# A decode attention kernel: K of each block in one transfer through three slots, the middle slot transposed first

## The chip, the cores and the metric

The kernel runs on one core of a Trainium2 chip. The core has a matrix engine (PE, with its weight loads listed as PEld), a vector engine (DVE), a scalar engine (ACT), a general engine (POOL, hardly used here) and a sync engine (SP) that issues the transfers from HBM; 16 DMA engines carry them. Each engine works through its own instructions in order and waits on semaphores for the others. The metric is the device time of one execution in microseconds; before the change it is 1268.74 us, the median of three runs (1267.89 to 1269.64).

## What is computed

One query token goes through a gated sum of two branches. Branch A is attention with 16 query heads over 8 K/V heads, 65,536 cached positions each, head size 256, and a product with `wo`. Branch B is a small mixer (layer norm, gelu, two vectors `w1`, `w2`). Cut to what matters:

```python
g = sigmoid((x * gate_w).sum(-1, keepdims=True))
q = (x @ wq).reshape(1, 1, 16, 256).transpose(0, 2, 1, 3)
k = repeat(k_cache, 2, axis=1); v = repeat(v_cache, 2, axis=1)
scores = einsum("bhqd,bhkd->bhqk", q, k) * 256 ** -0.5
o = einsum("bhqk,bhkd->bhqd", softmax(scores), v)
a = o.transpose(0, 2, 1, 3).reshape(1, 1, 4096) @ wo
u = gelu(einsum("bsd,sf->bdf", layernorm(x), w1) + b1)
b = (einsum("bdf,fs->bds", u, w2) + b2).transpose(0, 2, 1)
return g * a + (1 - g) * b
```

All arrays are bfloat16. K and V together are 537 MB, and each of their bytes is used by the two query heads of one K/V head only.

## The kernel before

The caches are cut into 32 blocks of 16,384 positions (8 MB of K and 8 MB of V each), four blocks to a K/V head. A position's row lies on one of 128 partitions; each partition holds 128 positions of a block, 64 KB of K and 64 KB of V, contiguous in HBM.

Per block: K lies in two tiles of 32 KB per partition, `kn0` and `kn1` (`k_tiles`), V in one tile `vt` of 64 KB. DVE transposes K in eight steps of 16 positions (`transposes`, line 384) into one of two tiles `kT`; after each step PE makes eight matmuls with the query placed in `qz` (`scores`, line 392) and gathers the scores of the block in one PSUM tile. After the eighth, `softmax` (line 444) follows on DVE, PE and ACT: the block's maximum, the running maximum, the exponentials `p_sb`, their transposition `pT`, the running sum `lsum` (line 488). Then 64 matmuls of `products` (line 412) multiply `pT` with V, and `accumulate` (line 493) adds them to `acc`.

The blocks 0 to 29 run in a loop of 15 passes of two blocks each, `e` = 0 and 1 (line 560). Every pass also loads one row set of `wo` (224 KB, `load_wo`) into `wo_sb[:, 1]`. At the end of the odd block, `denominators` and `head_end` turn `acc` into a head's output, multiply it with `wo_sb`, and ACT copies `wo_sb[:, 1]` to `wo_sb[:, 0]`; `turn` switches constants. `place_q` puts the next pair's query in place in the odd block's softmax. The blocks 30 and 31 are written out after the loop (line 581): their transfers are cut into pieces, and the last block's V goes into the K tiles in eight pieces (`load_v_last`), the last of which are small; its products are split between PE matmuls of two forms (`pv` into `pv_last`, and `columns`, line 437), and the result is multiplied with `wo_sb` (line 639).

The function `seq` fixes the order of each engine's instructions as written. All large transfers are issued by SP in program order into one queue, which the DMA engines serve in order. The order in a pass is V of the even block, K halves of the odd block, `wo`, V of the odd block, K halves of the next even block. An issue of K waits until the transposes have read the tile half that it overwrites; an issue of V waits until the products of the block before have read `vt`.

The loop uses staggered semaphores: its body has four stages, parted by `tc.stage_boundary()`, and an engine may enter a stage only when every engine has signalled that it is done with the stage two before. An engine signals this at the start of the following stage, unless the program names an earlier place with `tc.previous_stage_wait(engine)`; the kernel before names none. Stage 0 holds the even block's transposes, scores and V load, stage 1 its softmax and products and the next K loads; stages 2 and 3 hold the same for the odd block. SP passes through these stages like the others, so its K loads of stage 1 wait for all engines' signals about stage 3, and so on.

Before the loop, the query is made from `wq` (which lies in `vt` for that time), and the mixer's 14 gelu rows `gel` lie in the two `kT` tiles.

Of the kernel before, what the change touches and what calls it, by code (L numbers as in the profile page):

```python
# [8 lines left out]
FP32 = mybir.dt.float32  # L9
# [22 lines left out]
def kernel(  # L32
# [28 lines left out]
    def seq(ins):  # L61
        e = ins.ins.engine
        if e in last:
            tc.add_manual_dep(
                ins.ins,
                last[e],
                mybir.DependencyInfo(
                    mybir.DependencyClass.NoSync, mybir.DependencyReason.DATA
                ),
                reason="program order",  # L70
            )
        last[e] = ins.ins.name
        return ins
# [4 lines left out]
    psum = ctx.enter_context(tc.tile_pool(name="psum", bufs=1, space=bass.MemoryType.PSUM))  # L78


    kvpool.tile([128, 4096 - 128], mybir.dt.uint8, name="fill")
    k_tiles = [kvpool.tile([128, KP, DH], BF16, name=f"kn{i}") for i in range(2)]
    vt = kvpool.tile([128, VP, DH], BF16, name="vt")
    kT_tiles = [kvpool.tile([128, NJ, NW, 32, 2], BF16, name=f"kT{i}") for i in range(2)]
    p_sb = work.tile([128, 512], BF16)
    pT_tiles = [work.tile([128, 512], BF16, name=f"pT{i}") for i in range(2)]
    wo_sb = const.tile([128, REP, 2, D], BF16)
# [21 lines left out]
    gel = [  # L109
        kT_tiles[b % 2][:].rearrange("p j w k c -> p (j w k c)")[:, b // 2 * D:(b // 2 + 1) * D]  # L110
        for b in range(NF)
    ]

    flat = {}
    for name, cache in (("k", A_k_cache), ("v", A_v_cache)):
# [2 lines left out]
    def rows(name, n):  # L118
        return flat[name][bass.ds(n, 1)].rearrange("o p j d -> (o p) j d")

    def load_k(n, h, pieces=((0, KP),)):
        for j0, j1 in pieces:
            seq(nc.sync.dma_start(
                out=k_tiles[h][:, j0:j1, :],
                in_=rows("k", n)[:, h * KP + j0:h * KP + j1, :],
            ))

    def load_v(n, j0=0, j1=VP):
        seq(nc.sync.dma_start(out=vt[:, j0:j1, :], in_=rows("v", n)[:, j0:j1, :]))  # L129

    def pairs(ap):
        return ap.rearrange("p (i j) d -> p i j d", i=2)

    LAST = ((0, 32), (32, 64), (64, 80), (80, 96), (96, 112), (112, 120), (120, 124), (124, 128))

    def load_wo(h, r):
        seq(nc.sync.dma_start(
            out=wo_sb[:, r],
            in_=A_wo.rearrange("(h p c) n -> h p c n", p=128, c=2)[bass.ds(h, 1)].rearrange(
                "o p c n -> (o p) c n"  # L140
            ),
        ))

    def load_v_last(n):
        for j0, j1 in LAST:
            seq(nc.sync.dma_start(  # L146
                out=k_tiles[j0 // KP][:, j0 % KP:(j1 - 1) % KP + 1, :],
                in_=rows("v", n)[:, j0:j1, :],
            ))

# [5 lines left out]
    with nc.allow_non_contiguous_dma(reason="short rows"):  # L156
# [78 lines left out]
    sdev = work.tile([128, 1], FP32)  # L235
    rstd = work.tile([128, 1], FP32)
    ntmp = work.tile([128, 1], FP32)
    xf = work.tile([128, D], FP32)
    h_bc = work.tile([128, D], FP32)
    w1f = const.tile([128, NF], FP32)  # L240
    b1f = const.tile([128, NF], FP32)
    seq(nc.vector.tensor_copy(out=xf[:], in_=sm_ps[:, 0:D]))
    seq(nc.vector.bn_stats(out=stats[:], in_=xf[:]))
# [8 lines left out]
    for _ in range(2):  # L252
# [4 lines left out]
        ))  # L257
        seq(nc.vector.tensor_tensor(out=rstd[:], in0=rstd[:], in1=ntmp[:], op=ALU.mult))
    seq(nc.vector.tensor_scalar(
        out=h_bc[:], in0=xf[:], scalar1=mv[:, 0:1], scalar2=rstd[:, 0:1],  # L260
        op0=ALU.subtract, op1=ALU.mult,
    ))
    for b in range(NF):
        seq(nc.scalar.activation(
            out=gel[b], in_=h_bc[:], func=ACT.Gelu_apprx_tanh,
            scale=w1f[:, b:b + 1], bias=b1f[:, b:b + 1],
        ))

# [42 lines left out]
            ))  # L311

    place_q(0)
    zt = work.tile([1, D], FP32)
    z = const.tile([1, 1], FP32)
    ez = const.tile([1, 1], FP32)
    gate = const.tile([1, 1], FP32)
# [2 lines left out]
    rest = const.tile([1, D], FP32)  # L320

    def gate_sum():
        seq(nc.vector.tensor_tensor(out=zt[:], in0=xf[0:1, :], in1=gw[:], op=ALU.mult))
        seq(nc.vector.tensor_reduce(out=z[:], in_=zt[:], op=ALU.add, axis=AXIS.X))
        seq(nc.scalar.activation(out=ez[:], in_=z[:], func=ACT.Exp, scale=-1.0))

    def mixer_sum():
# [52 lines left out]
            out=ends[:], in0=ends[:], scalar1=-1.0, scalar2=1.0, op0=ALU.mult, op1=ALU.add  # L380
        ))

    def transposes(i):
        seq(nc.vector.transpose(  # L384
            out=kT_tiles[i % 2][:].rearrange("p j w k c -> p (j w k c)").bitcast(FP32),
            in_=k_tiles[i // 4][:, i % 4 * NJ:(i % 4 + 1) * NJ, :].rearrange("p j d -> p (j d)").bitcast(FP32),
        ))

    def scores(e, i):
        for w in range(NW):  # L390
            for c in range(2):
                seq(nc.tensor.matmul(  # L392
                    sc_tiles[e][:, :],
                    lhsT=qz[:, 2 * w + c, 2 * (NI - i):2 * (NI - i) + 128],
                    rhs=kT_tiles[i % 2][:, :, w, :, c],
                    start=(i == 0 and w == 0 and c == 0),
                    stop=(i == NI - 1 and w == NW - 1 and c == 1),
                ))
# [34 lines left out]
    def columns(j0, j1):  # L433
        for j in range(j0, j1):
            i, jj = divmod(j, NJ)
            for c in range(2):
                seq(nc.tensor.matmul(
                    o_last[:, c, :],
                    lhsT=k_tiles[j // KP][:, j % KP, :].rearrange("p (d c) -> p c d", c=2)[:, c, :],
                    rhs=pT_tiles[L % 2][:, 32 * jj + REP * i:32 * jj + REP * (i + 1)],  # L440
                    start=(j == KP and c == 0), stop=(j == VP - 1), skip_group_check=True,
                ))
# [176 lines left out]

    for ip in range(2):  # L620
        pv(L, ip, tile=k_tiles[0][:, 32 * ip:32 * (ip + 1), :], dst=pv_last, last_ip=1)
    accumulate(L % 2, pv_last)
    columns(64, 80)
    for c in range(2):
# [53 lines left out]
```

## Time and profile before

| what | value |
|---|---|
| median of three runs | 1268.74 us |
| the profiled execution's own time | 1268.93 us |
| its span (first to last instruction) | 1267.1 us |
| bytes read from HBM, rate over the span | 544.45 MB, 430 GB/s |
| PE busy | 806.4 us (64%) |
| DVE busy | 707.7 us (56%) |
| ACT busy | 58.6 us (5%) |
| mean granted PE clock | 0.807 |
| score matmuls, line 392 | 2048, 419 ns each |
| K transposes, line 384 | 256, 2283 ns each |
| product matmuls, line 412 | 1968, 526 ns each |
| K loads in halves (4 MB) | 63, median 27.3 us from issue to landing |
| V loads (8 MB) | 30, median 31.1 us from issue to landing |
| `wo` loads (224 KB) | 17, median 27.3 us from issue to landing |

The span lies inside the time of the execution; some 1.8 us lie around it. Matmuls overlap in the array, so the mean of one is longer than the distance between two. A landing time counts from the issue, so it holds the wait for the transfers ahead in the queue. In a row of the timeline the columns are start, duration, engine, line, operation, output and inputs, count, and in brackets the idle time before it with what ended it.

### The profile page before, as it was taken

How to read it: one execution, taken by the hardware profiler on the slowest of the kernel's cores; microseconds unless marked ns; L12 is line 12 of the kernel's file. 1: busy time of each engine (PE TensorE's matmuls, PEld its weight loads, DVE VectorE, ACT ScalarE, POOL GpSimd, SP SyncE). 2: the span in 40 equal slices, each digit the busy share in tenths (PEclk: the TensorE clock that was granted, in tenths of full speed). 3: DMA queues.
4: the chain of work that ended last, by engine and by line, in shares of the span. 5: the costliest groups of instructions: out<-in, count | busy, mean ns of one | idle time of the engine just before them, and what ended most of it. 6: DMA issues, size and time to landing. Idle time of an engine off the chain costs nothing.

```text
span 1267.1 us, 12204 instructions
## 1 busy us (share of the span) xinstructions
PE 806.4 (64%) x4689; PEld 321.2 (25%) x4689; DVE 707.7 (56%) x754; ACT 58.6 (5%) x131; POOL 1.7 (0%) x7
## 2 busy tenths in 40 slices
PE   3767665766656566566675675755657665676676
PEld 1222222222222222222222222222222222222223
DVE  4566545565445665456654556644566544665483
ACT  4000000000000000000000000000000000000000
POOL 0000000000000000000000000000000000000000
PEclk9888778788778787787877788777888778787687
DMA  9999999999999999999999999999999999999998
GB/s 413 414 437 444 429 439 418 435 432 446 434 418 437 431 450 432 432 420 432 449 432 435 418 433 434 445 435 418 438 430 447 435 430 424 430 446 435 418 419 343
DMA packets 18306, 544.59 MB, mean 430 GB/s; under 512 B 2421, under 2 KB 4600, under 8 KB 5112
## 3 DMA queue, kind: packets, MB, share of 16 engines
q1 hardware_dynamic: 17858, 544.45, 99.6%
q8 instruction: 6, 0.10, 0.0%
q10 hardware_dynamic: 438, 0.01, 0.0%
q14 instruction: 4, 0.03, 0.0%
HBM read 544.45 MB, written 0.00 MB: 430 GB/s over the span
## 4 chain that ended last, share of the span: by engine, by line
DMA 75%; issue 18%; PE 2%; DVE 2%; SPq 1%; ACT 0%; DVEq 0%
DMA vt<-in_A_v_cache_dram 73%; DMA kn<-in_A_v_cache_dram 2%; DVE kT L384 1%; PE sc L392 1%; PE pv_ps L412 1%; SPq L560 0%; SPq L129 0%; PE hd_ps L528 0%; PE f L639 0%; ACT p_sb L480 0%; DVE acc L493 0%; SPq L146 0%; DVE rmax L449 0%; DVE y_sb L339 0%; PE hd_ps L514 0%
## 5 line engine op out<-in xcount | busy, mean ns | idle before, releaser
L392 PE MATMUL sc<-kT,qz 128*128 128x512 bf16 x2048 | 550.9, 419 | 217.3 <-DVE kT L384 217.1
L384 DVE STREAM_TRANSPOSE kT<-kn 128x2048 f32<-128x2048 f32 x256 | 571.2, 2283 | 109.4 <-DMA kn<-in_A_k_cache_dram 52.6
L392 PEld LDWEIGHTS <-qz 128*128 128x128 bf16 x2048 | 212.7, 104 | 556.1 <-issue 379.4
L412 PE MATMUL pv_ps<-vt,pT 128*4 128x512 bf16 x1968 | 172.5, 526 | 129.0 <-DMA vt<-in_A_v_cache_dram 127.2
L493 DVE SCALAR_TENSOR_TENSOR acc<-acc,al,pv_ps 128x512 f32<-128x512 f32 x31 | 23.2, 748 | 266.5 <-PE pv_ps L412 266.5
L412 PEld LDWEIGHTS <-pT 128*4 128x4 bf16 x2000 | 58.7, 108 | 235.1 <-issue 190.0
L480 ACT ACTIVATE p_sb<-sc,nb 128x512 bf16<-128x512 f32 x32 | 22.0, 687 | 975.6 <-DVE nb L476 975.6
L449 DVE TENSOR_REDUCE rmax<-sc 128x1 f32<-128x512 f32 x32 | 22.1, 692 | 63.6 <-PE sc L392 63.6
L487 DVE STREAM_TRANSPOSE pT<-p_sb 128x512 bf16<-128x512 bf16 x32 | 22.8, 711 | 27.1 <-ACT p_sb L480 27.1
L499 PE MATMUL hd_ps<-lsum,same 128*128 128x1 f32 x30 | 7.4, 315 | 28.8 <-DVE lsum L488 28.8
L467 PE MATMUL sm_ps<-mrun,ones_f 1*128 1x2 f32 x64 | 12.1, 256 | 21.2 <-DVE mrun L466 12.9
L453 PE MATMUL sm_ps<-ident_f,rmax 128*1 128x128 f32 x32 | 8.6, 270 | 24.5 <-DVE rmax L449 24.5
L533 ACT COPY wo_sb<-wo_sb 128x896 bf16<-128x896 bf16 x15 | 14.1, 937 | 199.1 <-PE hd_ps L528 199.1
L514 PE MATMUL hd_ps<-esc,acc 128*128 128x2 f32 x60 | 9.5, 263 | 14.1 <-DVE acc L493 14.1
L528 PE MATMUL hd_ps<-wo_sb,oT 128*1 128x448 bf16 x60 | 17.9, 393 | 0.0
L532 DVE TENSOR_TENSOR a_acc<-a_acc,hd_ps 1x448 f32<-1x448 f32 x15 | 9.1, 608 | 14.5 <-PE hd_ps L528 14.5
L467 PEld LDWEIGHTS sm_ps<-mrun,ones_f 1*128 1x128 f32 x64 | 9.4, 182 | 27.4 <-DVE mrun L466 16.3
L499 PEld LDWEIGHTS hd_ps<-lsum,same 128*128 128x128 f32 x30 | 6.1, 253 | 30.1 <-DVE lsum L488 30.1
L514 PEld LDWEIGHTS hd_ps<-esc,acc 128*128 128x128 f32 x60 | 8.2, 196 | 21.6 <-DVE acc L493 21.6
L476 DVE CUSTOM_DVE_ANT_0 junk<-sm_ps,nval 128x2 f32<-128x2 f32 x32 | 5.1, 160 | 14.0 <-PE sm_ps L467 14.0
L453 PEld LDWEIGHTS sm_ps<-ident_f,rmax 128*1 128x1 f32 x32 | 2.5, 79 | 40.2 <-DVE rmax L449 40.2
L308 DVE COPY qz<-qq 32x16 bf16 (+1 forms) x64 | 10.5, 164 | 1.4
(114 smaller groups left out, 149.5 us busy)
## 6 DMA issues: line engine op xcount, KB each, us to landing
kn<-in_A_k_cache_dram SPq DMA_DIRECT2D x63, 4096.0 KB, 27.3
vt<-in_A_v_cache_dram SPq DMA_DIRECT2D x1, 5120.0 KB
kn<-in_A_k_cache_dram SPq DMA_DIRECT2D x2, 2048.0 KB, 11.9
kn<-in_A_v_cache_dram SPq DMA_DIRECT2D x2, 2048.0 KB, 20.9
wo_sb<-in_A_wo_dram SPq DMA_DIRECT2D x17, 224.0 KB, 27.3
vt<-in_A_wq_dram SPq DMA_DIRECT2D x1, 3072.0 KB, 10.3
vt<-in_A_v_cache_dram SPq DMA_DIRECT2D x1, 3072.0 KB
kn<-in_A_v_cache_dram SPq DMA_DIRECT2D x3, 1024.0 KB, 20.4
```

The source lines that it names most:

```text
L384: seq(nc.vector.transpose(out=kT_tiles[i % 2][:].rearrange("p j w k c -> p (j w k c)").bitcast(FP32), in_=k_tiles[i // 4][:, i % 4 * NJ:(i ...
L392: seq(nc.tensor.matmul(sc_tiles[e][:, :], lhsT=qz[:, 2 * w + c, 2 * (NI - i):2 * (NI - i) + 128], rhs=kT_tiles[i % 2][:, :, w, :, c], star ...
L412: seq(nc.tensor.matmul(dst[32 * grp:32 * grp + 2 * REP, :, :], lhsT=pT[:, 32 * jj + 2 * REP * ip:32 * jj + 2 * REP * (ip + 1)], rhs=pairs( ...
L449: seq(nc.vector.tensor_reduce(out=rmax[:], in_=sc_ps[:, :], op=ALU.max, axis=AXIS.X))
L467: seq(nc.tensor.matmul(sm_ps[:, 128:128 + REP], lhsT=ones_f[0:1, :], rhs=mrun[0:1, :], start=True, stop=True))
L480: seq(nc.scalar.activation(out=p_sb[:, :], in_=sc_ps[:, :], func=ACT.Exp, scale=scale, bias=nb[:, 0:1], accum_out=den[:, 0:1],))
L487: seq(nc.vector.transpose(out=pT[:, :], in_=p_sb[:, :]))
L493: seq(nc.vector.scalar_tensor_tensor(out=acc[:], in0=acc[:], scalar=al_tiles[e][:, 0:1], in1=src[:, :, :], op0=ALU.mult, op1=ALU.add,))
L499: seq(nc.tensor.matmul(hd_ps[:, 460:461], lhsT=same[:].rearrange("p a r -> p (a r)"), rhs=lsum[:, 0:1], start=True, stop=True,))
L514: seq(nc.tensor.matmul(o_ps[c], lhsT=acc[:, e, :].rearrange("p (d c) -> p c d", c=2)[:, c, :], rhs=weights[:, e, :], start=(start and e == ...
L528: seq(nc.tensor.matmul(a_ps, lhsT=oT[:, c, r:r + 1], rhs=wo_sb[:, r, c, :], start=(r == 0 and c == 0), stop=(r == REP - 1 and c == 1),))
L533: seq(nc.scalar.copy(out=wo_sb[:, 0], in_=wo_sb[:, 1]))
```

## The change

K now has 96 KB per partition: one tile `k_all` with three slots of 32 KB. An even block lies in slots 0 and 1, an odd block in slots 1 and 2. Each block in the loop is loaded by one transfer of 8 MB (`load_k_whole`) in place of two. An even block transposes slot 1 first and then slot 0 (`UPPER_FIRST`), an odd block slot 1 and then slot 2, so that slot 1, the middle one, is free after four transposes in both. The start and stop flags of the score matmuls follow that order.

The signals between the stages are placed by name: in stages 0 and 2, ACT's before the block and PE's and DVE's after the first step of transposes and scores; in stages 1 and 3, DVE's and ACT's after the softmax and PE's after the first quarter of the products.

Room for the third slot is made by laying the early values (`gel`, `xf`, `h_bc`, `zt`) into slot 2, and `wo_sb` into the padding in front of the K tile. Before the loop, block 0 is loaded with slot 1 first (in two pieces) and slot 0 second.

After the loop, block 30 lies in slots 0 and 1 and is transposed slot 1 first; block 31's first half goes to slot 2 and its second half to slot 1; block 31's V pieces go to slots 0 and 2. The mixer's tail and the gate's column come after block 30's softmax in place of between its transposes. Only head 15's rows of `wo` are loaded at the end; head 14's stay from the loop's last copy.

```diff
-    k_tiles = [kvpool.tile([128, KP, DH], BF16, name=f"kn{i}") for i in range(2)]
+    k_all = kvpool.tile([128, 3 * KP, DH], BF16, name="k_all")
+    slots = [k_all[:, i * KP:(i + 1) * KP, :] for i in range(3)]
...
+    early = slots[2].rearrange("p j d -> p (j d)")
+    gel = [early[:, b * D:(b + 1) * D] for b in range(NF)]
...
+    def load_k_whole(n, slot):
+        seq(nc.sync.dma_start(out=k_all[:, slot * KP:(slot + 2) * KP, :], in_=rows("k", n)))
...
+    v_half = [slots[0], slots[2]]
...
-    load_k(0, 0, ((0, 32), (32, KP)))
-    load_k(0, 1)
+    load_k(0, 1, 1, ((0, 32), (32, KP)))
+    load_k(0, 0, 0)
...
+    FORWARD = tuple(range(NI))
+    UPPER_FIRST = FORWARD[NI // 2:] + FORWARD[:NI // 2]
...
-    def score_block(e, hooks={}):
-        for i in range(NI):
-            transposes(i)
-            scores(e, i)
-            if i in hooks:
-                hooks[i]()
+    def score_block(e, pair, hooks={}, order=FORWARD):
+        for k, i in enumerate(order):
+            transposes(pair, i)
+            scores(e, i, k == 0, k == NI - 1)
+            if k in hooks:
+                hooks[k]()
...
     def products(e):
         for ip in range(NI // 2):
             pv(e, ip)
+            if ip == 0:
+                tc.previous_stage_wait(mybir.EngineType.PE)
         accumulate(e)
...
+    def early_signals(i):
+        def both():
+            tc.previous_stage_wait(mybir.EngineType.PE)
+            tc.previous_stage_wait(mybir.EngineType.DVE)
+        return {i: both}
+
     with tc.For_i(0, HQ - 1, 1, iteration_sync="staggered") as t:
         for e in range(2):
             if e:
                 tc.stage_boundary()
-            score_block(e)
+            tc.previous_stage_wait(mybir.EngineType.Activation)
+            score_block(
+                e, (e, e + 1), early_signals(0), FORWARD if e else UPPER_FIRST
+            )
             load_v(2 * t + e)
             tc.stage_boundary()
-            load_k(2 * t + e + 1, 0)
-            load_k(2 * t + e + 1, 1)
             if e == 0:
+                load_k_whole(2 * t + 1, 1)
                 load_wo(t, 1)
                 softmax(e, may_begin=True)
+                tc.previous_stage_wait(mybir.EngineType.DVE)
+                tc.previous_stage_wait(mybir.EngineType.Activation)
                 products(e)
             else:
+                load_k_whole(2 * t + 2, 0)
                 softmax(e, pair=t + 1)
+                tc.previous_stage_wait(mybir.EngineType.DVE)
+                tc.previous_stage_wait(mybir.EngineType.Activation)
                 denominators()
                 products(e)
                 head_end()
...
         if n < L:
-            score_block(n % 2, {1: mixer_tail, 2: gate_column})
+            score_block(0, (0, 1), order=UPPER_FIRST)
         else:
-            score_block(n % 2, {1: result_base, 2: lambda: pv(L - 1, 0), 3: lambda: pv_one(L - 1, 2)})
+            score_block(1, (2, 1), {1: result_base, 2: lambda: pv(L - 1, 0), 3: lambda: pv_one(L - 1, 2)})
         if n == L - 1:
             load_v(n, 0, 48)
-            load_k(L, 0)
-            load_k(L, 1)
+            load_k(L, 0, 2)
+            load_k(L, 1, 1)
             load_v(n, 48, VP)
         else:
             load_v_last(L)
-            for h in range(HQ - REP, HQ):
-                load_wo(h, h - (HQ - REP))
+            load_wo(HQ - 1, 1)
         if n < L:
             softmax(n % 2)
+            mixer_tail()
+            gate_column()
```

More of the change, by code (lines that the diff above doesn't have):

```diff
@@ L78 @@
     psum = ctx.enter_context(tc.tile_pool(name="psum", bufs=1, space=bass.MemoryType.PSUM))
-    kvpool.tile([128, 4096 - 128], mybir.dt.uint8, name="fill")
-    k_tiles = [kvpool.tile([128, KP, DH], BF16, name=f"kn{i}") for i in range(2)]
+    wo_sb = kvpool.tile([128, REP, 2, D], BF16, name="wo_sb")
+    kvpool.tile([128, 4096 - 128 - REP * 2 * D * 2], mybir.dt.uint8, name="fill")
+    k_all = kvpool.tile([128, 3 * KP, DH], BF16, name="k_all")
+    slots = [k_all[:, i * KP:(i + 1) * KP, :] for i in range(3)]
     vt = kvpool.tile([128, VP, DH], BF16, name="vt")
@@ L108 @@
     wq_t = vt[:, 48:56, :].rearrange("p a b -> p (a b)")
[L109 to L112, printed above, removed]
+    early = slots[2].rearrange("p j d -> p (j d)")
+    gel = [early[:, b * D:(b + 1) * D] for b in range(NF)]
+    early_f = early[:, NF * D:].bitcast(FP32)
+    xf, h_bc, zt = [early_f[:, i * D:(i + 1) * D] for i in range(3)]
+    zt = zt[0:1, :]
     flat = {}
@@ L146, in load_v_last @@
             seq(nc.sync.dma_start(
-                out=k_tiles[j0 // KP][:, j0 % KP:(j1 - 1) % KP + 1, :],
+                out=v_half[j0 // KP][:, j0 % KP:(j1 - 1) % KP + 1, :],
                 in_=rows("v", n)[:, j0:j1, :],
@@ L237 @@
     ntmp = work.tile([128, 1], FP32)
-    xf = work.tile([128, D], FP32)
-    h_bc = work.tile([128, D], FP32)
     w1f = const.tile([128, NF], FP32)
     b1f = const.tile([128, NF], FP32)
-    seq(nc.vector.tensor_copy(out=xf[:], in_=sm_ps[:, 0:D]))
-    seq(nc.vector.bn_stats(out=stats[:], in_=xf[:]))
+    seq(nc.vector.tensor_copy(out=xf, in_=sm_ps[:, 0:D]))
+    seq(nc.vector.bn_stats(out=stats[:], in_=xf))
     seq(nc.vector.bn_aggr(out=mv[:], in_=stats[:]))
@@ L259 @@
     seq(nc.vector.tensor_scalar(
-        out=h_bc[:], in0=xf[:], scalar1=mv[:, 0:1], scalar2=rstd[:, 0:1],
+        out=h_bc, in0=xf, scalar1=mv[:, 0:1], scalar2=rstd[:, 0:1],
         op0=ALU.subtract, op1=ALU.mult,
@@ L264 @@
         seq(nc.scalar.activation(
-            out=gel[b], in_=h_bc[:], func=ACT.Gelu_apprx_tanh,
+            out=gel[b], in_=h_bc, func=ACT.Gelu_apprx_tanh,
             scale=w1f[:, b:b + 1], bias=b1f[:, b:b + 1],
@@ L313 @@
     place_q(0)
-    zt = work.tile([1, D], FP32)
     z = const.tile([1, 1], FP32)
@@ L322, in gate_sum @@
     def gate_sum():
-        seq(nc.vector.tensor_tensor(out=zt[:], in0=xf[0:1, :], in1=gw[:], op=ALU.mult))
-        seq(nc.vector.tensor_reduce(out=z[:], in_=zt[:], op=ALU.add, axis=AXIS.X))
+        seq(nc.vector.tensor_tensor(out=zt, in0=xf[0:1, :], in1=gw[:], op=ALU.mult))
+        seq(nc.vector.tensor_reduce(out=z[:], in_=zt, op=ALU.add, axis=AXIS.X))
         seq(nc.scalar.activation(out=ez[:], in_=z[:], func=ACT.Exp, scale=-1.0))
@@ L381, in turn, with transposes, scores @@
         ))
-    def transposes(i):
+    FORWARD = tuple(range(NI))
+    UPPER_FIRST = FORWARD[NI // 2:] + FORWARD[:NI // 2]
+    def transposes(pair, i):
         seq(nc.vector.transpose(
             out=kT_tiles[i % 2][:].rearrange("p j w k c -> p (j w k c)").bitcast(FP32),
-            in_=k_tiles[i // 4][:, i % 4 * NJ:(i % 4 + 1) * NJ, :].rearrange("p j d -> p (j d)").bitcast(FP32),
+            in_=slots[pair[i // 4]][:, i % 4 * NJ:(i % 4 + 1) * NJ, :].rearrange("p j d -> p (j d)").bitcast(FP32),
         ))
-    def scores(e, i):
+    def scores(e, i, begin, end):
         for w in range(NW):
@@ L395, in scores @@
                     rhs=kT_tiles[i % 2][:, :, w, :, c],
-                    start=(i == 0 and w == 0 and c == 0),
-                    stop=(i == NI - 1 and w == NW - 1 and c == 1),
-                ))
-    def score_block(e, hooks={}):
-        for i in range(NI):
-            transposes(i)
-            scores(e, i)
-            if i in hooks:
-                hooks[i]()
+                    start=(begin and w == 0 and c == 0),
+                    stop=(end and w == NW - 1 and c == 1),
+                ))
+    def score_block(e, pair, hooks={}, order=FORWARD):
[4 more added lines that the diff above has]
+                hooks[k]()
     def pv(n, ip, jjs=range(NJ), tile=None, dst=pv_ps, last_ip=NI // 2 - 1):
@@ L620 @@
     for ip in range(2):
-        pv(L, ip, tile=k_tiles[0][:, 32 * ip:32 * (ip + 1), :], dst=pv_last, last_ip=1)
+        pv(L, ip, tile=v_half[0][:, 32 * ip:32 * (ip + 1), :], dst=pv_last, last_ip=1)
     accumulate(L % 2, pv_last)
```

7 lines of the change are left out of this document (3 added, 4 removed).

## The prediction

> **What bounds the kernel now.** I read the page's DMA rows first, then the chain of waits, then the sync queue's timeline of one loop pass, then DVE and PE in the same window, and last the first and the last block.
>
> ```profile
> DMA  9999999999999999999999999999999999999998
> q1 hardware_dynamic: 17858, 544.45, 99.6%
> DMA 75%; issue 18%; PE 2%; DVE 2%; SPq 1%; ACT 0%; DVEq 0%
> ```
>
> The 16 DMA engines are busy from the first slice to the last, and the chain is three quarters transfers. Counted from the trace's packet records, fewer than 16 packets are in flight for 0.14 us (mean over the engines) at 49 to 51 us, for 0.64 us at 1207 to 1209 us, and otherwise not at all between 4 and 1261 us. So the time is the sum of the transfers, plus a start, plus an end. PE (64%) and DVE (56%) only matter where they hold a transfer back or come after the last one.
>
> Whether they hold one back is read from one pass (blocks of 8 MB K and 8 MB V):
>
> ```profile
> 412.37 0.33 SPq L129 DMA_DIRECT2D vt<-in_A_v_cache_dram  x1
> 433.31 0.94 SPq L123 DMA_DIRECT2D kn<-in_A_k_cache_dram  x2
> 449.02 0.33 SPq L129 DMA_DIRECT2D vt<-in_A_v_cache_dram  x1
> 471.64 0.89 SPq L123 DMA_DIRECT2D kn<-in_A_k_cache_dram  x2
> 490.58 0.33 SPq L129 DMA_DIRECT2D vt<-in_A_v_cache_dram  x1
> ...
> 452.07 4.51 DVE L384 STREAM_TRANSPOSE kT<-kn 128x2048 f32<-128x2048 f32 x2 [2.72 <-DMA kn<-in_A_k_cache_dram]
> 477.09 0.18 DVE L488 SCALAR_TENSOR_TENSOR lsum<-lsum,al,den 128x1 f32<-128x1 f32 x1
> ```
>
> The trace's landing events give: the two K halves of this block at 452.05 and 461.75, its V at 481.62. The V issued at 449.02 had 12.7 us of K still ahead of it. From the first half landing to the softmax's last DVE row is 477.27-452.05 = 25.2 us.
>
> **K as one transfer, 30 times in the loop.** Medians of the landing intervals (mean over the 16 engines): half K 9.680 us (57 of them), whole V 19.319 us (27), wo 0.566 us (15). A whole K has V's shape (64 KB rows), so it saves 2x9.680-19.319 = 0.041 us; 30 times, 1.25 us. The packet records bound it above: 32 KB packets last 1213 ns, 64 KB ones 2418, and each transfer ends with one of 9 ns per engine; 8x(2x1213-2418)+9 = 73 ns, 2.2 us in all. The lower bound is nothing, if row length doesn't matter. I take 1.3, near the landings, which are what consumers wait for.
>
> **What the whole transfer costs.** The transposes now start when all 8 MB are in, 9.7 us later against the queue. The block's V waits for them only if its issue comes late. The trace of before has a block whose chain ran with its V already there, the first one:
>
> ```profile
> 27.77 4.50 DVE L384 STREAM_TRANSPOSE kT<-kn 128x2048 f32<-128x2048 f32 x2 [6.27 <-ACT ez L325]
> 52.83 6.29 PE L412 MATMUL pv_ps<-vt,pT 128*4 128x512 bf16 x64 [1.82 <-DVE pT L487]
> 59.68 0.33 SPq L129 DMA_DIRECT2D vt<-in_A_v_cache_dram  x1
> ```
>
> From first transpose to the next V's issue: 59.68-27.77 = 31.9 us, with PE at half clock for 13.7 us of it (granted clock 0.5 from 27.5 to 34.4 and from 51.4 to 58.3). An odd block adds place_q (0.75) and less than 1 us of denominators: at most 33.6. The queue must not be empty by then. The next K lands 19.32+19.36 = 38.7 us after this one; its fastest engine is 2.1 us ahead of its slowest (452.05 against 449.97 in the landings); a transfer that meets an idle queue moves its first packet 1.25 us after its issue (1207.16, first packet 1208.4). So the limit is 38.7-2.1-1.25 = 35.3 us. Spare 1.7 to 3.4 us: no gap, price zero; without that cover every microsecond beyond 35.3 is paid once per block, 30 times. The next K needs only the middle third: four transposes, some 11.5 us after landing (452.07 to about 463.5), while V fills the queue to 19.3. Its spare is 5 us or more.
>
> This holds only with the new early signals. Today K is issued at 471.64, after all eight transposes, and V at 490.58, 3.7 us after the products ended (486.9), when every engine had come round the loop. In the built order of the changed kernel the sync engine's waits ahead of each V and K are met by signals after the first score group (PE, DVE), after the softmax (DVE, ACT) and after a quarter of the products (PE). These signals are semaphore steps, and queued behind each are instructions that stand later in the chain anyway: nothing added beyond a few tens of ns.
>
> **The first block.** K of block 1 lands 10.00 us (mean; 10.37 the last engine) after V instead of 9.69, because its issue at 47.60 waited for all eight transposes. Four are done at about 39.5. Gain 0.3 to 0.7; I take 0.5. The gelu rows move into the unused third; block 1's K waits for their readers, which end at 26.2.
>
> **The end.** Its rows now:
>
> ```profile
> 1207.16 9.10 SPq L123 DMA_DIRECT2D kn<-in_A_k_cache_dram  x2
> 1221.55 4.50 DVE L384 STREAM_TRANSPOSE kT<-kn 128x2048 f32<-128x2048 f32 x2
> 1247.96 1.03 PE L412 MATMUL pv_last<-kn,pT 128*4 128x512 bf16 x16
> 1252.61 1.61 PE L412 MATMUL pv_last<-kn,pT 128*4 128x512 bf16 x16 [3.61 <-DMA kn<-in_A_v_cache_dram]
> 1255.91 1.84 PE L626 MATMUL hd_ps<-fst,acc 128*128 128x2 f32 x8
> 1262.80 0.37 PE L437 MATMUL hd_ps<-pT,kn 128*128 128x2 bf16 x8 [0.24 <-DMA kn<-in_A_v_cache_dram]
> 1263.42 1.04 PE L639 MATMUL f<-wo_sb,oT 128*1 128x224 bf16 x8 [0.25 <-DVE oT L633]
> ```
>
> The last block's first K half, issued at 1207.16 after block 30's fourth transpose, met an empty queue: it landed 10.84 after the piece of V before it, 1.16 over 9.68. It now goes to the unused third and needs no transpose: 1.16 gained on the transfers. Dropping head 14's wo takes 0.57 off the queue, but behind the last V piece; on the path it takes only the wait of L639's second half, which began at 1263.93 when that wo landed and could have begun at 1263.70: 0.23.
>
> By the transfers alone, the last V piece (1262.75 now) lands at 1262.75-1.3-0.5-1.16 = 1259.8. But PE has 3.6 us of slack before it (row 1252.61), and block 30 starts 9.7 us later against the queue. Its K lands at 1192.70+9.68-1.3-0.5 = 1200.6. Then 25.2 to the softmax's end, mixer_tail and gate_column, moved behind it, 2.1+0.16 on DVE (1198.07 to 1200.17 now): block 31's transposes start at 1228.1 (1221.55 now). To the first pv_last 26.4 as now: 1254.5. The 32 products without a wait 1.8 (0.205 per four, last one 0.38), accumulate 0.85: 1257.2. The eight L626 0.94 at full clock (0.1175 each, as L514) or 1.71 at half; 96 matmuls of L437 at 0.0267, 2.56: they end at 1260.85, now 1263.17. So PE, not the transfer, ends last, by 0.8 us. Sum: 1263.17-1260.85 = 2.3, plus 0.23, less 0.2 for a last engine that landed 0.45 behind at 1202.83: 2.3 us. The span 1267.1 becomes 1264.8. The profiled run is 1268.93 (1.8 around its span), 0.2 above the median of the runs: 1266.5 against 1268.74.
>
> **A rule of the skill.** The Trainium skill (DMA: Bandwidth & Descriptors, "Anatomy of one DMA") fits a transfer as some 2.0 us fixed plus its bytes at 436 GB/s, for gpsimd's path. By it, paid in turn, 30 transfers fewer would be 60 us; the trace speaks against it here, where halves land 9.68 apart.
>
> **The rivals.**
> - *The queue runs dry (slower).* A V that still waits for the loop's turn, as at 490.58, is issued 3.7 us later than at most 33.6: 37.3 against 35.3, a gap of 2 us in each of 15 odd blocks: +30-2, 1297; at the chain's lower value (31.9) only 0.3 each, 1271. For it: the odd block's long end. Against: the built order and the first block. 8%.
> - *The transfers end last.* If PE's end chain is a microsecond shorter than I add up, 1259.8 holds: last landing to end 4.39-0.23, span 1264.0, 1265.6. For it: PE has no idle to cool in. 20%.
> - *Row length saves nothing and PE is at half clock at the end:* K at 1201.9 and 0.77 more end L437 at 1262.9, the span at 1266.7; with the 0.45 at 1267.1, no change. 1267.5 (one of the two) to 1268.8. For it: L626 ran at 0.213 each, the half-clock price. 18%.
> - *Each transfer pays a fixed price:* at the 1.25 of an idle start, 37 us less, 1230. Against: 0.041, measured. 1%.
>
> **How the numbers follow.** Forecast 53%. No change means within 0.2% (2.5 us), about what a measurement of this kernel can tell. The forecast's 2.3 stands beside that bound, and medians of three scatter by some 0.6 (runs 1267.89 to 1269.64), so a little under half of it counts as faster: 0.24, plus 0.16 of the second rival and 0.01 of the fourth: 0.41. Slower 0.08, the rest 0.51. Range: from the transfers' end with the packet bound (1265.6 less 0.9) to no gain: 1264.6 to 1268.7; what is left out is mostly the dry queue.
>
> **What would show it.** K landings 38.6 us apart with V in between at 19.3 and no gap; V issued 32 to 34 us after K's landing; the queue's issues of K some 11 to 12 us after it; no empty queue near 1207; PE busy without a DMA wait from 1228 to the end. It is wrong if a V is issued later than 35 us after its K, if the whole K does not land in 19.32, or if PE waits for the last V piece.

## The result, and the profile after

| | before | after |
|---|---|---|
| median | 1268.59 us (19 runs, 1267.14 to 1270.06) | 1266.36 us (19 runs, 1265.91 to 1267.15) |
| ratio after/before | | 0.9983, 95% interval 0.9976 to 0.9989 |
| profiled execution, its span | 1268.93, 1267.1 us | 1266.01, 1264.2 us |
| K landing in the loop, median | 9.680 us for each half | 19.31 us for the whole |
| one pass of the loop | 77.945 us | 77.845 us |
| `wo` loads, packets of q1 | 17, 17858 | 16, 13394 |

The change makes the kernel 2.2 us faster, about as much as forecast (2.3). The profiled execution of after lies at the fast end of its runs and that of before above its median, so the span fell by 2.9. In the page of after, the row of the DMA engines, the queue and the chain of waits:

```profile
DMA  9999999999999999999999999999999999999998
q1 hardware_dynamic: 13394, 544.22, 99.6%
DMA 69%; DVE 12%; PE 12%; issue 4%; SPq 0%; DVEq 0%; ACT 0%
```

The transfers still fill the span. New are DVE and PE in the chain, 12% each, where "issue" had 18%: the chain runs over the transposes and scores of blocks, since every block now waits for its whole K. That is no cost by itself; the queue decides. One pass in the timeline of after (sync queue, then DVE; columns as before):

```profile
432.98 0.33 SPq L131 DMA_DIRECT2D k_all<-in_A_k_cache_dram  x1
451.09 0.33 SPq L134 DMA_DIRECT2D vt<-in_A_v_cache_dram  x1
471.12 0.33 SPq L131 DMA_DIRECT2D k_all<-in_A_k_cache_dram  x1
491.61 0.33 SPq L134 DMA_DIRECT2D vt<-in_A_v_cache_dram  x1
...
460.85 4.50 DVE L390 STREAM_TRANSPOSE kT<-k_all 128x2048 f32<-128x2048 f32 x2 [9.01 <-DMA k_all<-in_A_k_cache_dram]
485.63 0.18 DVE L494 SCALAR_TENSOR_TENSOR lsum<-lsum,al,den 128x1 f32<-128x1 f32 x1
```

The landing events put K at 422.18 and 460.83 and V at 441.49 and 480.71: K lands every 38.65 us with V in between. The next K is issued 10.8 and 10.3 us after a K has landed, V 28.9 us (451.09) and 30.8 us (491.61) after it. Over all such issues in the loop from 80 us on it is 10.3 to 11.5 us for K and 28.9 to 33.2 for V. From a landing (460.83) to the start of the softmax's last row it is 24.8 us. Between 60 and 1150 us fewer than 16 packets are in flight for less than 0.001 us in all. And in the list of waits of after (total, times, longest):

```profile
DVE kT L390 <- DMA k_all<-in_A_k_cache_dram: 164.4, 30, 12.4
PE pv_ps L418 <- DVE pT L493: 27.2, 15, 1.8
```

DVE waits for every K, up to 12.4 us, and PE no longer waits for V in the loop (before, it waited 127.2 us for it in 29 blocks): V is always there before its products.

The end of after, in the timeline:

```profile
1198.16 0.34 SPq L134 DMA_DIRECT2D vt<-in_A_v_cache_dram  x1
...
1227.92 4.48 DVE L390 STREAM_TRANSPOSE kT<-k_all 128x2048 f32<-128x2048 f32 x2
...
1254.31 1.90 PE L418 MATMUL pv_last<-k_all,pT 128*4 128x512 bf16 x32
1257.07 1.10 PE L648 MATMUL hd_ps<-fst,acc 128*128 128x2 f32 x8
1258.03 2.66 PE L443 MATMUL hd_ps<-pT,k_all 128*128 128x2 bf16 x96
1260.95 0.69 PE L661 MATMUL f<-wo_sb,oT 128*1 128x224 bf16 x8 [0.26 <-DVE oT L655]
```

From the first `pv_last` to the last of line 443 no row names a wait for a transfer; before, PE stood for V pieces in four rows of that form. The records of the single matmuls show a short one inside the last row: they start 0.025 us apart, but the last eight begin at 1260.338, 0.131 after the one before them and 0.05 after the last V piece's landing (1260.29). So in this execution PE's chain and the last piece end within 0.1 us of each other, the piece later. Landings at the end (last of the 16 engines; in brackets the mean interval since the landing above):

```
                         before             after
K(30)                    1202.83            1200.73
V(30), first 48 of 128   1210.07 ( 7.25)    1208.05 ( 8.30)
K(31), first half        1220.13 (10.84)    1218.66 ( 9.77)
K(31), second half       1229.71 ( 9.88)    1228.33 ( 9.67)
last piece of V(31)      1262.75            1260.29
```

Two things stand there that the forecast did not have: the first piece of V(30) came 1.05 us late in the mean of the engines, and the last V piece still held the end, if by 0.1 us. (The last engine was 1.47 us behind the mean at K(30) and only 0.48 behind at that piece, after an empty queue. So its own landing looks on time, 7.32 after K(30), and the delay shows at K(31).)

### The profile page after: what moved, and what is told of

Its sections match the earlier page's. It is cut to its first block, busy times and chain, and to the rows that moved or that the text cites. A ratio compares the mean times of both kernels' runs of the same rounds, so it can differ in the third digit from the quotient of the medians.

```text
span 1264.2 us, 12020 instructions
## 1 busy us (share of the span) xinstructions
PE 799.8 (63%) x4689; PEld 317.3 (25%) x4689; DVE 707.4 (56%) x754; ACT 58.6 (5%) x131; POOL 1.7 (0%) x7
## 3 DMA queue, kind: packets, MB, share of 16 engines
q1 hardware_dynamic: 13394, 544.22, 99.6%
## 4 chain that ended last, share of the span: by engine, by line
DMA 69%; DVE 12%; PE 12%; issue 4%; SPq 0%; DVEq 0%; ACT 0%
DMA k_all<-in_A_k_cache_dram 67%; DVE kT L390 12%; PE sc L398 12%; DMA k_all<-in_A_v_cache_dram 2%; PE hd_ps L443 0%; PE pv_last L418 0%; SPq L131 0%; PE hd_ps L648 0%; ACT p_sb L486 0%; PE f L661 0%; DVE rmax L455 0%; DVE y_sb L342 0%; DVEq L390 0%; DVE rest L348 0%; DVE rest L345 0%
## 5 line engine op out<-in xcount | busy, mean ns | idle before, releaser
L390 DVE STREAM_TRANSPOSE kT<-k_all 128x2048 f32<-128x2048 f32 x256 | 570.8, 2282 | 221.0 <-DMA k_all<-in_A_k_cache_dram 164.4
## 6 DMA issues: line engine op xcount, KB each, us to landing
k_all<-in_A_v_cache_dram SPq DMA_DIRECT2D x3, 1024.0 KB, 22.3
```

The source lines that it names most:

```text
L390: seq(nc.vector.transpose(out=kT_tiles[i % 2][:].rearrange("p j w k c -> p (j w k c)").bitcast(FP32), in_=slots[pair[i // 4]][:, i % 4 * N ...
```

## The experiments

Theory: the gain is the row length of K in the queue plus a shorter end; the early signals and the middle slot give nothing themselves but keep the queue full. At the very end PE's own chain sets the time. Rivals: the signals are the gain; the row length is nothing; the transfers set the end. Each kernel is the changed one with the edit shown, unless said otherwise.

**K in halves and in quarters.** All else stays: three slots, order, signals.

```diff
-        seq(nc.sync.dma_start(out=k_all[:, slot * KP:(slot + 2) * KP, :], in_=rows("k", n)))
+        step = VP // 2        # second kernel: VP // 4
+        for j in range(0, VP, step):
+            seq(nc.sync.dma_start(
+                out=k_all[:, slot * KP + j:slot * KP + j + step, :],
+                in_=rows("k", n)[:, j:j + step, :],
+            ))
```

> The changed kernel, with each K block of the loop in two transfers of 4 MB again (slots, order and signals stay). Theory (long rows land faster: two passes of the loop took 77.95 us a pass before and 77.84 after, so 0.054 us per K): the pass goes back to 77.95, K landings in two steps of 9.68, and the kernel is 1.6 us slower than the changed one, 1268.0. Rival (row length is worth nothing, the gain lies in the earlier issue at the first block and at the end): pass 77.84, 1266.4.

> The changed kernel, with each K block of the loop in four transfers of 2 MB (16 KB rows): the suspected price of shorter rows made larger. Theory: by the packet records 16 KB last 611 ns and 64 KB 2418, 8x(4x611-2418)+27 = 235 ns per K; at the 0.74 that the halves showed of that (0.054 of 0.073), 0.174 us per K, 5.2 us in all, 1271.6 (4 to 7 more). Rival: 1266.4.

Measured: halves 1267.49 us (10 runs; 0.9993 of before, 0.9983 to 1.0002), quarters 1268.80 (10 runs; 1.0003, 0.9994 to 1.0013). The halves are 0.77 us below the kernel before on the same chip, where the changed kernel is 2.23 below. A pass takes 77.845, 77.931 and 78.108 us with one, two and four transfers per K: 0.043 us per K for the cut into two, 0.13 for the cut into four, over 30 K 1.29 and 3.95 us. K(30) lands at 1200.73, 1201.96 and 1204.26. The cut changes the length of the rows and the number of transfers together, so these figures stand for both; by the packet records in the forecast 64 of 73 ns lie in the rows. The gain is in the queue, and it is worth what the forecast said.

The quarters' time was expected too high. 0.174 us per K was assumed and 0.13 measured, and V(30) met no empty queue: its first piece landed 7.26 us after K(30) in place of 8.30, so that the last V piece came at 1262.78, 2.5 us later than in the changed kernel and not 3.5. PE's chain is early there, because block 30's transposes begin when three quarters of K(30) are in (the third landed at 1199.57), so PE waits for V pieces and the last one sets the end. One row of the halves, then two of the quarters:

```profile
1259.27 2.67 PE L448 MATMUL hd_ps<-pT,k_all 128*128 128x2 bf16 x96
...
1199.67 4.50 DVE L395 STREAM_TRANSPOSE kT<-k_all 128x2048 f32<-128x2048 f32 x2 [6.16 <-DMA k_all<-in_A_k_cache_dram]
1260.34 1.01 PE L448 MATMUL hd_ps<-pT,k_all 128*128 128x2 bf16 x32 [1.49 <-DMA k_all<-in_A_v_cache_dram]
```

With halves V(30) met no empty queue either, and the last V piece came at 1260.30, as in the changed kernel (1260.29); the span grew by 1.5 all the same. PE's row of 96 ends 1.26 later (1261.95 after 1260.69), and the last product took 0.91 us instead of 0.69, at a granted clock of 0.50. So there the later K(30), and PE's chain behind it, moved the end, not the last V piece.

**The signals alone.** The kernel before, with the named signals and nothing else of the change:

```diff
+            tc.previous_stage_wait(mybir.EngineType.Activation)
-            score_block(e)
+            score_block(e, early_signals(0))
...
+                tc.previous_stage_wait(mybir.EngineType.DVE)
+                tc.previous_stage_wait(mybir.EngineType.Activation)
...
+            if ip == 0:
+                tc.previous_stage_wait(mybir.EngineType.PE)
```

> The kernel before, with the early signals between the stages added and nothing else. Theory (the queue of the kernel before is never empty in the loop but once, at the first block): K's first half is issued after four transposes instead of eight, the gap at 49 to 51 us goes, 0.2 to 0.5 us less, 1268.3; the empty queue at 1207 stays. Rival (the signals are the gain): as the changed kernel, 1266.4.

Measured: 1268.02 us (10 runs) beside 1268.26 for the kernel before on the same chip, 0.9996 (0.9986 to 1.0005): no difference that can be told. A pass takes 77.931 us, as with the halves. The empty queue of the first block shrinks to 0.01 us, that at the end from 0.64 to 0.20 us; it had been expected to stay.

**No signals, and no middle slot first.** The changed kernel without its named signals (no `previous_stage_wait` is left), and, as a second kernel, with them but with both blocks transposed in ascending order:

```diff
-                e, (e, e + 1), early_signals(0), FORWARD if e else UPPER_FIRST
+                e, (e, e + 1), early_signals(0), FORWARD
```

> The changed kernel without the early signals (stages signal where they begin). Theory (they are the cover of the late landing): K is issued after all eight transposes, 19.6 us after the K before it landed (471.64 against 452.05 before), while V is in at 19.3 on the slowest engine and 17.2 on the fastest; with 1.25 us from issue to first packet the queue is empty for 2.5 to 3.7 us in each of 30 blocks: 75 to 110 us more, 1340 to 1375. Rival (the queue is deep enough anyway): 1266.4.

> The changed kernel, with the even blocks of the loop transposed in plain order (slot 0, then slot 1). Theory (the middle third first is what lets the next K be issued in time): the K of an odd block then waits for all eight transposes of the even one, some 19.5 us after its landing, and the queue is empty for 2.5 to 3.7 us in 15 blocks: 37 to 55 us more, 1304 to 1322; the odd blocks' issues stay at 11.5 us. Rival (the order is of no account): 1266.4.

Measured: 1351.29 us without signals (1.0652, 1.0631 to 1.0673; two runs), 1311.62 without the order (1.0340, 1.0322 to 1.0359; two runs), both inside what was expected. The page and the timeline of the kernel without signals:

```profile
q1 hardware_dynamic: 13394, 544.22, 94.7%
```

```profile
441.47 0.33 SPq L134 DMA_DIRECT2D vt<-in_A_v_cache_dram  x1
467.66 0.33 SPq L131 DMA_DIRECT2D k_all<-in_A_k_cache_dram  x1
...
453.86 13.28 DVE L390 STREAM_TRANSPOSE kT<-k_all 128x2048 f32<-128x2048 f32 x6 [1.34 <-PE sc L398]
```

K landed at 447.92, V at 467.20, and only then, when the eighth transpose had ended (453.86+13.28 = 467.14), came the next K at 467.66. It landed 22.3 us after that V in place of 19.3. Each block pays that: passes take 83.711 us, and the queue is empty for 58.2 us between 60 and 1150 us. Without the order it happens only after the even block, where the middle slot is free after eight transposes instead of four: between 400 and 500 us the next K is issued 20.2 us after an even block's K has landed (437.53, 457.71) and 10.9 after an odd block's. Passes take 80.887 us, with 28.5 us of empty queue. So the whole transfer loses 83 us against the kernel before without the signals, and 44 without the order. Both together cost nothing that can be told, as the kernel with halves shows, which has them and not the whole transfer (0.9993 of before).

**The end: head's end, mixer, both.** The changed kernel leaves V(30) late and puts 2.2 us of mixer on DVE ahead of block 31's transposes. Three kernels: the mixer's tail and the gate's column ahead of block 30's transposes; the odd block's `head_end` at the start of the next pass (a first one on zeros, the last one after the loop); both.

```diff
         if n < L:
+            mixer_tail()
+            gate_column()
             score_block(0, (0, 1), order=UPPER_FIRST)
...
             softmax(n % 2)
-            mixer_tail()
-            gate_column()
```

```diff
             tc.previous_stage_wait(mybir.EngineType.Activation)
+            if e == 0:
+                head_end()
...
-                head_end()
                 turn()
+    head_end()
     last.clear()
```

> The changed kernel, with the mixer's tail and the gate's column ahead of block 30's transposes, in the 2.6 us in which DVE waits for K. Theory (two bounds stand within 0.1 us of each other at the end: the last V piece lands at 1260.29, PE's own chain ends at 1260.69 where the piece alone would let it end at 1260.56): block 31 starts 2.2 us earlier and PE waits for the V pieces again; 0.1 us less, 1266.2. Rival (PE alone sets the end): 2.2 us less, 1264.2.

> The changed kernel, with head_end moved over the loop's turn: the output of a pair is made at the start of the next pass (the first pass adds a zero, a last one follows the loop), so the loop is left some 3 us earlier. Theory (the 1.05 us by which the first V piece after the loop lands late, 8.30 against 7.25, come from the barrier after the last head_end): that gap goes, V pieces land 1.05 us earlier, but PE's chain from K's landing stays: 0 to 0.1 us less, 1266.3. Rival (the transfers set the end): 1.05 less, 1265.3.

> Both edits: mixer's tail ahead of block 30 and head_end over the loop's turn. Theory (two bounds, each within 0.1 us of the other): together they give what neither gives alone, 1.0 to 1.2 us less, 1265.3, with PE waiting for the last V piece. Rival (the gap is not the barrier's, or the end is something else): the sum of what they gave alone.

| kernel | median, runs | minus before on its chip | ratio to before | V(30) issued | last V piece | span |
|---|---|---|---|---|---|---|
| changed kernel | 1266.36, 19 | -2.23 | 0.9983 (0.9976 to 0.9989) | 1198.16 | 1260.29 | 1264.2 |
| mixer | 1266.75, 11 | -1.18 | 0.9990 (0.9980 to 0.9999) | 1199.08 | 1261.13 | 1265.3 |
| head's end | 1266.09, 11 | -1.84 | 0.9985 (0.9976 to 0.9994) | 1194.98 | 1258.79 | 1264.0 |
| both | 1264.80, 7 | -3.13 | 0.9971 (0.9960 to 0.9983) | 1193.03 | 1258.77 | 1262.9 |

The mixer's kernel did not do what its edit says. Its timeline:

```profile
27.66 0.67 DVE L342 TENSOR_SCALAR y_sb<-f,b2f 1x448 f32<-1x448 f32 x1
30.25 0.35 SPq L134 DMA_DIRECT2D vt<-in_A_v_cache_dram  x1
...
1258.50 0.99 PE L443 MATMUL hd_ps<-pT,k_all 128*128 128x2 bf16 x32 [1.34 <-DMA k_all<-in_A_v_cache_dram]
```

Nothing in the loop touches the mixer's tiles, and behind the loop `seq` starts a new order (`last.clear()`), so nothing held the tail there and it was put in front of the loop. The loop's first V is issued at 30.25 instead of 27.46, the queue is empty for 0.5 us between 30 and 32, and everything lands later (the last V piece by 0.84). At the end PE now stands for V pieces.

With the head's end in the next pass, V(30) finds a full queue (7.37 between K(30) and its first piece, mean of the engines), and the last V piece lands 1.5 us sooner. But the end stays:

```profile
1194.98 0.34 SPq L134 DMA_DIRECT2D vt<-in_A_v_cache_dram  x1
...
1258.07 2.54 PE L443 MATMUL hd_ps<-pT,k_all 128*128 128x2 bf16 x96
```

The row of 96 matmuls starts at 1258.07, as in the changed kernel (1258.03), and now runs through without the 0.1 us: it ends at 1260.61 in place of 1260.69. That is all that 1.5 us of transfers brought, since PE's own chain ends there; the rest of the 0.2 us of span is the last product, which took 0.55 us at a granted clock of 1.00 in place of 0.69. With both edits the mixer's tail stays behind the loop (line 342 starts at 1196.19), since `head_end`, which reads what the loop wrote, stands ahead of it. PE is early enough to wait again, 0.31 us for the last piece, and the time is 0.5 us below what was expected:

```profile
1193.03 0.34 SPq L134 DMA_DIRECT2D vt<-in_A_v_cache_dram  x1
...
1256.17 2.34 PE L443 MATMUL hd_ps<-pT,k_all 128*128 128x2 bf16 x88
1258.82 0.35 PE L443 MATMUL hd_ps<-pT,k_all 128*128 128x2 bf16 x8 [0.31 <-DMA k_all<-in_A_v_cache_dram]
```

**The mixer, held behind the loop.** The same edit with one copy that reads the running sum, which the loop writes:

```diff
         if n < L:
+            seq(nc.vector.tensor_copy(out=junk[:, 0:1], in_=lsum[:]))
             mixer_tail()
```

> The changed kernel with the mixer's tail and the gate's column ahead of block 30's transposes as in the run that moved them alone, but held behind the loop by one copy that reads the running sum (0.1 us on DVE). V(30) is still issued behind the head's end. Theory (two ends tie: PE's end chain and the last V piece are 0.1 us apart in the changed kernel): block 31's transposes start at 1225.8 instead of 1227.9, V(0) of the loop is issued at 27.5 again, the last V piece lands at 1260.3 as before the edit, PE waits for the V pieces at the end (some 2 us over the rows of line 443), the last of line 443 ends at 1260.6: span 1264.1, median 1266.2. Rival A (the late V(30) costs nothing at the last piece): as with both edits, span 1262.9, median 1264.8. Rival B (the 0.4 that the run with the mixer moved alone lost came from DVE's work ahead of the transposes, not from its place in front of the loop): last V piece at 1261.1, span 1265.3, median 1266.7.

Measured: 1265.08 us (8 runs, 1264.69 to 1265.61; 0.9975, 0.9965 to 0.9986), 3.20 below before on its chip. That is near rival A (1264.8), far from the theory (1266.2) and from rival B (1266.7). In its timeline:

```profile
1225.01 4.50 DVE L390 STREAM_TRANSPOSE kT<-k_all 128x2048 f32<-128x2048 f32 x2
...
1257.01 1.01 PE L443 MATMUL hd_ps<-pT,k_all 128*128 128x2 bf16 x32 [0.75 <-DMA k_all<-in_A_v_cache_dram]
1259.48 0.38 PE L443 MATMUL hd_ps<-pT,k_all 128*128 128x2 bf16 x8 [0.26 <-DMA k_all<-in_A_v_cache_dram]
```

Block 31's transposes start at 1225.01 (1227.92 in the changed kernel), and PE waits for V pieces, as the theory has it. But the last V piece landed at 1259.43, not at 1260.3: the exit of the loop took less in this execution. It is not a constant, as five profiled executions show:

| kernel | K(29) landed | products of block 29 | V(30) issued | after landing | queue empty | K(30) to V piece |
|---|---|---|---|---|---|---|
| two `wo` (below) | 1161.47 | 6.33 | 1198.51 | 37.0 | 0.87 | 8.85 |
| changed kernel | 1161.43 | 6.16 | 1198.16 | 36.7 | 0.51 | 8.30 |
| mixer | 1162.32 | 6.19 | 1199.08 | 36.8 | 0.22 | 8.14 |
| mixer, held | 1161.14 | 5.97 | 1197.42 | 36.3 | 0.10 | 7.87 |
| both | 1161.24 | 5.31 | 1193.03 | 31.8 | 0 | 7.28 |

(us; 64 matmuls of line 418; the empty time is the mean over the engines, 1150 to 1255; the last column is the mean interval to the first piece of V(30). In "both" `head_end` stands behind the issue.) The mean granted clock in these products was 0.56, 0.58, 0.58, 0.60 and 0.68 from the first row to the last: they take longer the more of them fall into half clock (last section), and V(30) goes out the later. So the assumption that failed is that the changed kernel's two ends, 0.1 us apart in one profile, are tied in every execution. The mixer's move alone lowers the time by about 1.0 us (3.20 against 2.23 below before). All its runs lie below all of the changed kernel's, but the two intervals against before overlap, so the size of that 1.0 is not sharp.

**Two rows of `wo` at the end.** Head 14's rows loaded once more ahead of head 15's, as before the change:

```diff
-            load_wo(HQ - 1, 1)
+            for h in range(HQ - REP, HQ):
+                load_wo(h, h - (HQ - REP))
```

> The changed kernel with both heads' rows of wo loaded at the end again, head 14's first; nothing else is changed. Theory (only the last product waits for it): the last V piece lands at 1260.3 as without it, wo 0.57 later, the row of line 661 takes 1.04 us instead of 0.69 and the span is 0.35 longer, 1264.55. Rival (a transfer at the end of the queue delays all that counts): the span is 0.57 longer or more, 1264.8.

The one run took 1267.09 us, with a span of 1265.3, 1.1 longer and not 0.35. The row that waits for the second `wo`, and below it the same row of the kernel "mixer, held", which loads one row set:

```profile
1261.62 1.03 PE L662 MATMUL f<-wo_sb,oT 128*1 128x224 bf16 x8 [0.25 <-DVE oT L656]
1260.11 0.91 PE L662 MATMUL f<-wo_sb,oT 128*1 128x224 bf16 x8 [0.26 <-DVE oT L656]
```

1.03 against the changed kernel's 0.69 is 0.34, as expected, but the second `wo` is not the whole of it. Both rows above ran at a granted clock of 0.50 throughout; in the profile of the changed kernel the clock was 1.00 until 1261.2, and the row began at 1260.95. At the same clock the second `wo` costs 0.12 us (1.03 against 0.91), and 0.22 is the clock. The rest stands ahead of that row, where this edit does nothing: the last V piece landed at 1260.95 instead of 1260.29, because this execution left the loop with 0.87 us of empty queue. The time, of one run, does not tell theory and rival apart.

## Why the prediction was right, and where it was not

- **What bounds it.** This was right: the time is the sum of the transfers, a start and an end. Between 60 and 1150 us the queue is empty for less than 0.001 us.
- **K as one transfer, 1.3 us.** A pass is 0.10 us shorter, 1.5 us over 15, and the cut into halves gives 1.29 back. Both lie inside the bounds of 0 and 2.2. K(30) landed at 1200.73, forecast 1200.6.
- **No gap in the loop.** V is issued 28.9 to 33.2 us after its K, forecast 32 to 34, against a limit of 35.3. K is issued 10.3 to 11.5 us after the landing, forecast 11.5. That the signals and the middle slot carry this is shown by the 83 and 44 us that are lost without them. One term of the limit was misread: the first packet of the K half issued at 1207.16 moved at 1208.13, not at 1208.4, so 0.97 us lie between them and not 1.25 (0.97 again at V(30) in after), and the limit is 35.6. Nothing hangs on it.
- **The first block, 0.5.** This term was too large: K(1) landed 0.24 us sooner (71.71 after 71.95; mean of the engines 0.11). The empty queue did go (0.139 to 0.004 us), but the whole K took 19.45 us there, where 19.31 is usual.
- **The end by the transfers, 1259.8: the step that failed.** Of the 1.16 us to be gained on the transfers 1.07 came (10.84 to 9.77 at K(31)). But the 35.3 us were checked for V's issues within the loop only, not for the one behind it. V(30) stands behind the loop's last pass and is issued when the engines have left it, `head_end` included: 36.7 us after K(29), beyond the 35 that the forecast had named as a sign of being wrong. It met an empty queue and gave 1.05 back. The landing of the last V piece was 1260.29. With `head_end` moved it is 1258.79.
- **PE ends last, by 0.8 us.** PE's steps held: transposes of block 31 at 1227.92 (forecast 1228.1), `pv_last` at 1254.31 (1254.5), the eight float32 matmuls at full clock in 1.10, the last of line 443 done at 1260.69 (1260.85). The 0.8 did not hold, because the last V piece came 0.5 later than forecast: in the profiled execution PE waited for it, 0.1 us, which the forecast had named as a sign that it is wrong. The medians speak for PE's chain as the end that counts: shortened alone it gave about 1.0 us, while the last V piece 1.5 us sooner, alone, gave nothing that could be told (0.9985 against 0.9983).
- **`wo`, 0.23.** This term was too large. The row of the last product fell from 1.04 to 0.69 us, but before ran it at a granted clock of 0.50 throughout. At that clock it takes 1.03 to 1.04 with head 14's rows and 0.91 without: `wo` is worth 0.12 to 0.13, and 0.22 of the 0.35 is the clock of the one profiled execution.
- **The sum, 2.3.** That 2.2 came out is in part luck. The first block and `wo` gave 0.4 us less than their terms, while K gave 0.2 more and PE's chain ended 0.16 sooner than added up. The late V(30) cost 0.1 us and not 1.05 in the profile, because PE's chain ends there almost as late as the last V piece lets it.
- **The rivals.** The dry queue did not come in the loop, but once behind it, for 0.5 us. "The transfers end last" holds in the one profile by 0.1 us, but not with the time of that rival (1265.6), and it is how the kernels with the mixer moved end. "Row length saves nothing" is refuted by the halves and quarters, and the eight float32 matmuls at the end started 0.1175 us apart, the full-clock price. A fixed price per transfer of 1.25 us is refuted: a second transfer in line costs 0.043.
- **Left open.** What the loop's late exit costs in a typical execution is not known. Between the profiles of "mixer, held" and "both" it is 0.7 us of span; between their medians, each against before on its chip (3.20 and 3.13), nothing. The profiles are one execution each, and the gap depends on the clock granted in it.

The kernels "both" and "mixer, held" beat the changed one. Their runs (1264.61 to 1264.99 and 1264.69 to 1265.61) all lie below the lowest of its 19 (1265.91). Part of that distance, 0.3 to 0.7 us, is the chips', by the kernel before on them.

## What to carry to other kernels

When a queue is the bound, sum what each transfer takes when it stands in line, and then go through every issue, the one behind a loop too, and ask whether it comes before the queue runs dry; an issue that is in time in the loop can be late at its exit. A larger transfer is only worth its gain if what frees its place and what lets it be issued come as early as for the smaller ones. An end at which two chains are tenths of a microsecond apart in one profile is not a tie: move each alone, and make sure that the moved work stays where it was put.

## What the runs showed of the hardware

- A transfer that stands in line costs next to nothing of its own: 8 MB in rows of 64 KB land in 19.31 us, in two of 32 KB 0.043 us later, in four of 16 KB 0.13 later. The Trainium skill (DMA: Bandwidth & Descriptors, "Anatomy of one DMA") gives 2.0 us fixed for a transfer on gpsimd's path; paid in turn on this queue that would be an estimate of 60 us for the 30 cuts, and the runs show 1.29.
- An empty queue costs more than its empty time. Where it was empty ahead of V(30) for 0.10, 0.22, 0.51 and 0.87 us (mean over the engines), the first piece landed 7.87, 8.14, 8.30 and 8.85 us after K(30). In the six other profiles with this order behind the loop and a full queue there (before, signals alone, halves, quarters, head's end, both) it was 7.25 to 7.37. Why each landing is later by 0.4 to 0.7 us more than the empty time is not shown.
- The same 64 product matmuls of line 418 took anything from 3.62 to 6.55 us in one execution. In two stretches of after (columns: window, length, busy time and count of PE, PEld, DVE, ACT and POOL, granted clock, DMA share, GB/s):

```profile
449.00:451.00 2.00, 1.97 (x40) 0.77 (x29) 0.00 (x0) 0.00 (x0) 0.00 (x0) 1.00 1.13 492
1188.50:1190.50 2.00, 2.00 (x24) 0.67 (x20) 0.00 (x0) 0.00 (x0) 0.00 (x0) 0.50 1.13 492
```

The counts take in those under way at the edges, and the last two columns count packets by their start, so that a share can pass 1. At a granted clock of 1.00 the 2 us hold 40 of the matmuls, at 0.50 only 24. The products from 447.34 (3.62) lie wholly in the first kind, those of block 29 (6.16) mostly in the second. Where the half clock falls differs from block to block and from one execution to the next, and it shifts the issue of V: for the even blocks from 28.9 us after the landing of K, where the products take 3.62, to 32.1, where they take 6.55.
